# Products of spectra in an H3 layer with SwiGLU: instructions of 2560 elements against 5120 with a repeated row

## The chip, the core and the metric

The kernel runs on one core of one Trainium2 chip. The time is the device time of one execution in microseconds; lower is better. The kernel before was run three times: 264.83, 265.25 and 281.7 us, median 265.25 us. The profile shows one further execution of its own.

## What is computed

A sequence of 2048 tokens with 640 channels goes through two layers, each behind a layer norm and with a residual. The first is an H3 layer: `k` goes through a causal filter of four taps and is multiplied with `v`; the product is convolved along the sequence with a filter as long as the sequence (by FFT in the reference), gets a skip term, and is multiplied with the normed `q`. The second is a SwiGLU of width 1728.

```python
k_shift = sum(k_pad[:, t:t + S, :] * shift_k[:, ks - 1 - t][None, None, :] for t in range(ks))
kv = k_shift * v
y_f = rfft(kv padded to 2S) * rfft(ssm_k padded to 2S)
y = irfft(y_f)[:S].astype(bfloat16) + kv * ssm_D
h = q + layernorm(q) * y
n = layernorm(h)
out = h + (silu(n @ w_gate) * (n @ w_up)) @ w_down
```

## The kernel before

The sequence is cut into four blocks of 512 tokens. For block j, `kv` and the filter's piece `g` are brought into an odd-frequency spectrum of length 1024 by matmuls with the cosine and sine matrix `WF` (`transform`; products in PSUM, taken out by ACT or DVE at L364, the upper half of the frequencies made by one DVE sum, L410 or L439 to L445). A spectrum is a tile `S` of 128 partitions x 2 x 4 x 640 in bf16: two halves of the frequencies, in each two rows of cosine and two of sine parts. `X[j]` is the spectrum of `kv`, `G[j]` that of the filter's piece. `window` joins `G[j]` and `G[j-1]` to `H[j]` in two sums; for block 2 one of them is a DMA with accumulation issued by POOL (`S<-S`, L279).

The output spectrum of block j is A = X[0]H[j] + X[1]H[j-1] + ... + X[j]H[0], with complex products. `mac` makes one of these: m03 stands for the product of X[0] for block 3, m13 for that of X[1], and so on. `inverse` brings A back by matmuls with `WI` (L874), a DVE instruction per row of 128 tokens multiplies by the normed `q` (L888), adds the residual (L901, or a POOL DMA for blocks 1 and 2) and takes the sum for the second norm. `turn_h` norms the rows (ACT L803 or DVE L800) and transposes them (by DMA for blocks 1 to 3, L915). Then comes the FFN of the block: gate and up products on PE (L986, L1063), silu and copy on ACT (L1046, L1052), their product on DVE (L1054, here called a gate), the product with `w_down` on PE (L1106), and, for blocks 0 to 2, an accumulating POOL DMA of each row of tokens into the output (L1113).

The first norm of blocks 0, 1 and 3 is computed by POOL in 14 small instructions (L759 to L783) from sums that ACT takes (L750, L792); POOL's queue also issues the accumulating DMAs (L279) and part of the weight loads (L955). All other loads and transposes are issued by SP.

Nothing is scheduled at run time. The program first lists some 925 operations with what they read and write; `ORDER` is a list of their numbers, and each engine's queue is what the list leaves of its operations, in that order. A number -n-1 takes the other engine for an operation that has one (an eviction on DVE in place of ACT, a load by POOL in place of SP). Buffers are handed out along the same list from the counts in `SLOTS`: 8 tiles `S`, 11 tiles `big` of 5120 bytes a partition (blocks of x, v, k and g, turned tiles, weights, and scratch `scr`), 5 rows `row`, 4 pairs of gate tiles `sg`, 4 PSUM tiles `ps`. A buffer's next user waits for its last reader.

`mac` in the kernel before, for the first product of a block (L721 to L726) and for the others (L729 to L741): `part(sin)` is the cosine (0) or sine (1) part of both halves, 2 x 1280 elements.

```python
# first: six instructions of 2560 elements
t = X.part(1) * H.part(1);  u = X.part(1) * H.part(0)
A.part(0) = X.part(0) * H.part(0);  A.part(1) = X.part(0) * H.part(1)
A.part(0) -= t;  A.part(1) += u
# others: four pairs of 2560 elements, b a scratch tile of big
for xs, hs, dst, f in ((0, 0, 0, add), (0, 1, 1, add), (1, 1, 0, sub), (1, 0, 1, add)):
    b = X.part(xs) * H.part(hs);  A.part(dst) = f(A.part(dst), b)
```

For m11, `ADDP` lets the second pair's sum be an accumulating DMA (`S<-big`, L279). The products of block 0 (m00) are made in two pieces of 1280 elements by the first form.

Of the kernel before, what the change touches and what calls it, by code (L numbers as in the profile page):

```python
# [52 lines left out]
MERGE = ()  # L53
# [55 lines left out]
SLOTS = {'S': 8, 'big': 11, 'kT': 0, 'tT': 1, 'row': 5, 'sg': 4, 'ps': 4, 'sm': 6}  # L109
# [104 lines left out]
def kernel(ctx: ExitStack, tc: tile.TileContext, A_q, A_k, A_v, A_shift_k, A_ssm_k, A_ssm_D, B_x,  # L214
# [6 lines left out]

    slots = SLOTS
    shape = {"S": ([P, 2, 4, D], BF16), "U": ([P, 2, 4, D], BF16), "big": ([P, R * D], BF16), "kT": ([P, KT, R, PAD + P], BF16), "tT": ([P, NC_FULL, BLK], BF16),
# [476 lines left out]
    def mac(A, X, H, first, pieces=((0, 1),), adds=(), at=None):  # L700

        if at in MERGE:
            merged(A, X, H, first, [a for a in adds if isinstance(a, int)])
# [619 lines left out]
```

## Time and profile before

| | |
|---|---|
| runs, us | 264.83, 265.25, 281.7 |
| profiled execution, us | 268.25 |
| its span, first to last instruction, us | 266.5 |
| PE, DVE, ACT, POOL busy, us | 252.7, 205.6, 170.1, 86.8 |
| granted TensorE clock | 1.00 in all slices |
| moved by DMA | 46.38 MB, of it 12.13 MB by POOL's queue |

The profile's times are those of the profiled execution, which took 268.25 us, 3.0 us more than the median of the runs. Busy times of one engine are a union: matmuls overlap, so their mean duration times their number is more than PE's busy time. Where a group's row has idle time, it is time in which its engine stood still ahead of it, with what ended most of it. In the timeline, a start of the next instruction ahead of the end of the one before is normal on DVE: the engine's instructions overlap at their ends.

### The profile page before, as it was taken

Reading aid. Unit: us, or ns where it says so; the run is one execution under the profiler, and the core shown is the slowest. Engines: PE = TensorE matmul, PEld = TensorE weight load, DVE = VectorE, ACT = ScalarE, POOL = GpSimd, SP = SyncE. Lnnn points to the kernel's source line nnn. Section 1 sums busy time; section 2 is a strip of 40 time slices with the busy share of each in tenths; the row PEclk is TensorE's granted clock in tenths of the full one; section 3 lists DMA queues with packets and bytes.
Section 4 is the critical chain, followed back from the end, with each engine's and each line's share of the span. In section 5 each row is a group of like instructions: output and inputs, shape, how many; then the busy total and the mean of one; then the engine's idle time right before and its main releaser. Section 6 shows DMA issues by size and latency. Waiting matters only on the chain.

```text
span 266.5 us, 4771 instructions
## 1 busy us (share of the span) xinstructions
PE 252.7 (95%) x1800; PEld 153.9 (58%) x1818; DVE 205.6 (77%) x300; ACT 170.1 (64%) x291; POOL 86.8 (33%) x121
## 2 busy tenths in 40 slices
PE   8999989899999969799999999999999999999994
PEld 8977566555764537565644467644446764444662
DVE  5689999999895998899999999999999601112222
ACT  4978999995786955988956993445567223344100
POOL 7970000159716020443214220099972013000000
PEclk9999999999999999999999999999999999999999
DMA  7997999799799999999998589685399635300002
GB/s 259 370 213 163 259 312 237 198 311 241 212 189 105 167 245 224 243 242 179 227 210 162 123 255 184 167 133 141 87 189 304 137 75 57 43 0 0 2 26 72
DMA packets 65730, 46.38 MB, mean 174 GB/s; under 512 B 31030, under 2 KB 61244, under 8 KB 65708
## 3 DMA queue, kind: packets, MB, share of 16 engines
q1 hardware_dynamic: 59906, 33.94, 53.9%
q0 software_dynamic: 5792, 12.13, 24.7%
q8 instruction: 14, 0.23, 0.4%
q14 instruction: 8, 0.07, 0.1%
q10 hardware_dynamic: 10, 0.01, 0.0%
HBM read 30.01 MB, written 4.59 MB: 130 GB/s over the span
## 4 chain that ended last, share of the span: by engine, by line
PE 32%; DVE 27%; DMA 12%; POOL 6%; issue 6%; ACT 2%; SPq 2%; DVEq 0%; POOLq 0%; ACTq 0%
PE ps L1106 15%; PE ps L986 13%; DMA S<-S 8%; DVE big L739 6%; DVE S L740 5%; DMA out_dram<-big 3%; PE ps L1063 3%; DVE S L712 3%; DVE row L888 2%; SPq L461 2%; DVE tT L1054 1%; DMA big<-in_B_w_gate_dram 1%; DVE big L712 1%; DVE S L822 1%; POOL sm L782 1%
## 5 line engine op out<-in xcount | busy, mean ns | idle before, releaser
L986 PE MATMUL ps<-big,big 128*128 128x512 bf16 x465 | 107.0, 379 | 1.1 <-ACT sg L1052 0.3
L986 PEld LDWEIGHTS <-big 128*128 128x128 bf16 x480 | 46.7, 98 | 52.6 <-issue 0.5
L1106 PE MATMUL ps<-wd,tT 128*128 128x320 bf16 (+2 forms) x416 | 60.6, 299 | 3.3 <-DVE tT L1054 1.4
L1106 PEld LDWEIGHTS <-tT 128*128 128x128 bf16 x416 | 40.5, 98 | 20.8 <-issue 2.3
L1046 ACT ACTIVATE sg<-ps 128x1024 bf16<-128x1024 f32 (+1 forms) x28 | 27.1, 969 | 33.7 <-PE ps L986 26.5
L375 PE MATMUL ps<-big,WF 128*128 128x320 bf16 x240 | 39.6, 299 | 2.5 <-ACT big L364 1.3
L740 DVE TENSOR_TENSOR S<-S,big 128x2560 bf16<-128x2560 bf16 x23 | 34.3, 1492 | 1.4 <-DMA S<-big 0.7
L739 DVE TENSOR_TENSOR big<-S,S 128x2560 bf16<-128x2560 bf16 x23 | 34.1, 1483 | 0.6 <-DMA out_dram<-big 0.6
L375 PEld LDWEIGHTS <-WF 128*128 128x128 bf16 x240 | 23.1, 97 | 15.5 <-issue 4.2
L1054 DVE TENSOR_TENSOR tT<-sg,sg 128x1024 bf16<-128x1024 bf16 (+1 forms) x25 | 16.0, 642 | 19.9 <-ACT sg L1052 19.9
L1052 ACT CAST sg<-ps 128x1024 bf16<-128x1024 f32 (+1 forms) x25 | 23.7, 948 | 6.6 <-PE ps L986 4.3
L750 ACT ACTIVATE row<-big 128x640 bf16<-128x640 bf16 x32 | 23.8, 749 | 5.3 <-DMA big<-in_A_q_dram 3.2
L364 ACT CAST S<-ps 128x320 bf16<-128x320 f32 (+1 forms) x38 | 19.9, 567 | 5.2 <-PE ps L375 4.8
L1113 POOL DMA_DIRECT2D out_dram<-row x12 | 12.0, 1078 | 24.9 <-ACT row L1112 24.9
L1112 ACT CAST row<-ps 128x640 bf16<-128x640 f32 x12 | 8.1, 696 | 17.0 <-PE ps L1106 16.6
L803 ACT ACTIVATE row<-big,sm 128x640 bf16<-128x640 bf16 x20 | 17.9, 920 | 0.0
L364 ACT ACTIVATE big<-ps 128x640 bf16<-128x640 f32 (+1 forms) x25 | 16.0, 669 | 2.6 <-PE ps L375 2.5
L955 POOL DMA_DIRECT2D big<-in_B_w_gate_dram x8 | 8.3, 1040 | 26.3 <-DVE S L740 10.8
L1063 PE MATMUL ps<-big,big 128*128 128x512 bf16 x57 | 14.4, 379 | 0.5 <-DVE row L888 0.3
L712 DVE TENSOR_TENSOR big<-S,S 128x2560 bf16<-128x2560 bf16 (+1 forms) x10 | 12.1, 1217 | 3.3 <-DMA S<-S 3.2
L279 POOL DMA_DIRECT2D big<-row x8 | 6.9, 863 | 21.4 <-DVE row L888 11.0
L874 PEld LDWEIGHTS <-WI 128*128 128x128 bf16 x96 | 9.2, 98 | 6.4 <-issue 1.1
(107 smaller groups left out, 327.8 us busy)
## 6 DMA issues: line engine op xcount, KB each, us to landing
big<-in_B_w_up_dram SPq DMA_DIRECT2D x17, 320.0 KB, 4.4
big<-in_B_w_gate_dram SPq DMA_DIRECT2D x16, 320.0 KB, 5.3
big<-in_A_q_dram SPq DMA_DIRECT2D x4, 640.0 KB, 5.7
big<-in_A_v_dram SPq DMA_DIRECT2D x4, 640.0 KB, 6.3
big<-in_A_ssm_k_dram SPq DMA_DIRECT2D x4, 640.0 KB, 7.9
big<-in_B_w_gate_dram POOLq DMA_DIRECT2D x8, 320.0 KB, 5.2
big<-in_B_w_up_dram POOLq DMA_DIRECT2D x7, 320.0 KB, 5.6
wd<-in_B_w_down_dram SPq DMA_DIRECT2D x1, 2080.0 KB, 13.7
```

The costliest lines, as they stand in the source:

```text
L364: (lambda: nc.scalar.activation(dst(), src(), ACT.Copy, scale=2.0)) if twice else (lambda: nc.scalar.copy(dst(), src())),
L375: nc.tensor.matmul(ap(ps)[:, h, 0:NH], w, ap(src)[:, r, h * NH:(h + 1) * NH], start=(first and i == 0), stop=(last and i == len(rs) - 1), ...
L712: return lambda: f(*(x() for x in args))
L739: nc.vector.tensor_mul(flat2(b), X.part(xs), H.part(hs))
L740: f(A.part(dst), A.part(dst), flat2(b))
L750: act(825, lambda r=r, junk=junk: nc.scalar.activation(ap(junk), ap(x)[:, r, :], ACT.Square, scale=D ** -0.5, accum_out=sm(s, 1)[:, r:r + ...
L986: nc.tensor.matmul(of(ps, i), ap(w)[:, k, off:off + P], ap(hT)[:, k, lo:lo + n], start=(k == 0), stop=(k == KT - 1))
L1046: act(1010 if wide else 600, lambda: nc.scalar.activation(of(sg), of(*gate), ACT.Silu), [(gate[0], gate[1] + i) for i in range(m)], [sg])
L1052: op = plan.add("act", 1010 if wide else 590, lambda: nc.scalar.copy(of(co), of(*up)), psu + [sg], [co] + tt, (), ("dve", 1230 if wide els ...
L1054: op.rest = dve(690 if wide else 420, lambda: nc.vector.tensor_mul(to(), of(sg), of(co)), [sg, co], tt)
L1063: nc.tensor.matmul(ap(ps)[:, i, :], ap(w)[:, k, off:off + P], ap(hT)[:, k, :], start=(k == 0), stop=(k == KT - 1))
L1106: nc.tensor.matmul(ap(ps)[:, hf, to:to + n], t, ap(wd)[:, c, col + (hf - hs[0]) * NH:col + (hf - hs[0]) * NH + n], start=(c == order[0]), ...
```

## The change

Three constants are changed. `MERGE` names the nine products of blocks 1 to 3, which so go through `merged` (in the program before too, but not called there). `SLOTS` gets one wide buffer `U` of 10240 bytes a partition, and two `big` fewer. `ORDER` is written anew, since the numbers change (925 operations become 924) and the sequence with them.

```diff
-MERGE = ()
+MERGE = ((1, 0), (1, 1), (2, 0), (2, 1), (2, 2), (3, 0), (3, 1), (3, 2), (3, 3))
...
 ORDER = [
-    1, 22, 0, 2, 4, 5, 6, 23, 25, 16, 3, 13, 7, 11, 26, 9, 28, 10, 12, 8, 14, 15, 27, 38, 17, 18, 19, 39, 36, 37, 134, 32, -34,
...
+    0, 2, 24, 1, 4, 5, 7, 10, 6, 23, 3, 13, 8, 14, 15, 11, 9, 16, 22, 12, 41, 19, 32, 38, 34, 20, 25, 33, 36, -40, 40, -38, 35,
...
-SLOTS = {'S': 8, 'big': 11, 'kT': 0, 'tT': 1, 'row': 5, 'sg': 4, 'ps': 4, 'sm': 6}
+SLOTS = {'S': 8, 'kT': 0, 'tT': 1, 'row': 5, 'ps': 4, 'sm': 6, 'big': 9, 'U': 1, 'sg': 4}
```

What `merged` does, shortened; `rows(b)` is the whole tile as 2 x 2 x 1280, and `by(sin)` is one part of X with each half's 1280 elements read twice by a step of 0:

```python
def by(sin):
    return lambda: X.part(sin).unsqueeze(2).broadcast_to([P, 2, 2, 2 * D])
def times(T, sin):                      # 5120 elements
    return lambda: v.tensor_mul(rows(T.b), by(sin)(), rows(H.b))
T = Spec(new("U"), H.swapped)
if first:
    times(T, 1);  times(A, 0)
else:
    U = Spec(new("U"), H.swapped);  times(U, 0)
    v.tensor_add(rows(A.b), rows(A.b), rows(U.b))      # rows(U.b)[:, :, ::-1] if A and H hold cosine and sine the other way round
    times(T, 1)
v.tensor_sub(A.part(0), A.part(0), T.part(1))          # 2560 elements
v.tensor_add(A.part(1), A.part(1), T.part(0))
```

So a first product has four instructions (T, A, two sums) and another one five (U, +U, T, two sums). `U` and `T` take turns in the one buffer. `merged` takes only whole numbers from `ADDP`, and the entry for m11 is a pair, so the sum of m11 is made by DVE and its DMA is gone.

The new order as the queues see it, from the end of the inverse of block 0 to m02 (numbers of the new program in brackets):

| queue | before | after |
|---|---|---|
| POOL | norm 0, pairs, copy L554, two `T<-T` (block 2), DMA sum of m11, norm 1, DMA sum of H2 | norm 0, one `T<-T` (block 1), pairs, copy L554 (399), norm 1 (278), DMA sum of H2 (434) |
| ACT | two of the eight sums for norm 1 among block 0, six behind the eviction of X1 and G2's first | all eight sums for norm 1 (270 to 277) between X0 and the kv rows of block 1 |
| DVE | norm, H1, m01 with X1's upper half, m11 with 3 gates, inverse 1 (L819), G2's upper half, L822, H2, gate, m02 among four L888 | H1, norm, m01 (261 to 264) with X1's upper half, G2's upper half (433), m11 U (265), H2 (435), +U, gate, T, two sums, gate, inverse 1 with kv rows of block 2 and two gates, three L888 and a gate, m02's A (466), the last L888, m02's T, gate, its sums |
| PE | G2 among FFN 0 | G2 ahead of FFN 0, but for one part |

Seven gates of FFN 0, 1 and 2 stand directly behind a 5120 in the new order: behind +U of m11, T of m02, U of m12, T of m03, +U of m13, +U and T of m33. The first loads of SP are in both k, x, v and g of block 0 and `WF`; then before: D, g1, x1, the minus matrices, k1; after: x1, g2, D, the minus matrices, g1, k1. The load of `w_down` (2080 KB) is issued ahead of k2 in place of behind it. POOL issues 5, 5 and 8 of the weight pieces of FFN 1, 2 and 3 in place of 7, 3 and 5.

72 rows, old and new, of the table ORDER are left out of this document.

## The prediction, made before the changed kernel was run

> **What bounds the kernel now.** I read the busy table and the 40 slices first, then the stages, then the chain that ended last.
>
> ```profile
> span 266.5 us, 4771 instructions
> PE 252.7 (95%) x1800; PEld 153.9 (58%) x1818; DVE 205.6 (77%) x300; ACT 170.1 (64%) x291; POOL 86.8 (33%) x121
> DVE  5689999999895998899999999999999601112222
> 20.00:120.00 100.00, 92.42 (x716) 58.06 (x722) 93.34 (x124) 82.76 (x149) 29.35 (x34) 1.00 1.06 223
> 120.00:218.00 98.00, 96.54 (x612) 55.18 (x619) 89.09 (x127) 60.32 (x93) 37.54 (x37) 1.00 0.78 175
> ```
>
> Columns of the stages: length, then busy time of PE, PEld, DVE, ACT, POOL. Two engines are full at once. DVE works without a break from 20 us to about 205 us and then is nearly done. PE is full all along; its idle time is 7.6 us between 20 and 120 us, 1.5 us between 120 and 218 us, and the start and the very end. The last third is PE alone (FFN of block 3), and it can't begin before the inverse transform of block 3 leaves DVE. So DVE's queue sets when PE's last part may start, and PE's idle time before that is all that any change on DVE can win: at most 7.6 us of 268.
>
> Where does DVE itself stand still? The chain shows it.
>
> ```profile
> 71.69 0.29 POOL sm L760
> 71.98 1.63 issue
> 73.62 13.26 DMA S<-S
> 86.91 1.49 DVE big L712
> ...
> DVE big L712 <- DMA S<-S: 3.2, 1, 3.2
> PE ps L1106 <- DVE tT L1054: 1.4, 2, 1.2
> PE ps L1106 <- ACT sg L1071: 1.2, 1, 1.2
> PE ps L471 <- DMA big<-in_A_ssm_k_dram: 1.2, 1, 1.2
> ...
> 96.79 0.72 PE L1106 MATMUL ps<-wd,tT 128*128 128x320 bf16 x4 [1.24 <-DVE tT L1054]
> 99.81 6.41 PE L1106 MATMUL ps<-wd,tT 128*128 128x320 bf16 x46 [1.22 <-ACT sg L1071]
> ```
>
> The one long stop of DVE behind the start-up is at 83.7 us: the second product of m02 needs H2, one half of which is an accumulating DMA (S<-S, line 279). That DMA was issued at 73.6 us, when the POOL norm of block 1 had ended (72.0 us) and DVE had made G2's upper half, and it took 13.3 us. DVE waits 3.2 us. PE's stalls on FFN 0's gates (L1054, L1071) lie right behind it, at 96 to 100 us.
>
> **The change part by part.** *The products.* Per non-first mac four pairs (product, sum) become U, +U, T of 5120 elements and two sums of 2560; per first mac six of 2560 become two and two. The elements are the same, except that the DMA sum of m11 comes back to DVE. So only the fixed share of an instruction can be won, for 24 fewer of them, and the price of that is in how close the starts stand, not in the durations.
>
> ```profile
> L740 DVE TENSOR_TENSOR S<-S,big 128x2560 bf16<-128x2560 bf16 x23 | 34.3, 1492 | 1.4 <-DMA S<-big 0.7
> L739 DVE TENSOR_TENSOR big<-S,S 128x2560 bf16<-128x2560 bf16 x23 | 34.1, 1483 | 0.6 <-DMA out_dram<-big 0.6
> L712 DVE TENSOR_TENSOR S<-S,big 128x1280 bf16<-128x1280 bf16 x4 | 3.1, 814 | 0.0
> L854 DVE TENSOR_TENSOR S<-big 128x1280 bf16<-128x1280 bf16 x4 | 3.1, 820 | 0.0
> ...
> 112.75 1.48 DVE L739 TENSOR_TENSOR big<-S,S 128x2560 bf16<-128x2560 bf16 x1
> 114.27 1.49 DVE L740 TENSOR_TENSOR S<-S,big 128x2560 bf16<-128x2560 bf16 x1
> 115.68 1.48 DVE L739 TENSOR_TENSOR big<-S,S 128x2560 bf16<-128x2560 bf16 x1
> ```
>
> 1280 elements take 0.814 us and 2560 take 1.483: 0.523 ns an element and 0.145 us fixed. So 5120 would take 1.483 + 2560 x 0.523 ns = 2.82 us. But starts follow each other after 1.41 us where the next does not need the result and after 1.52 us where it does (112.75, 114.27, 115.68). A pair costs 2.93, a mac of four pairs 11.72 us. With the same overlap a 5120 is followed after 2.75 us, or 2.85 us if waited for. U, +U and T are each waited for, because U and T share the one wide buffer: 3 x 2.85 + 1.41 + 1.52 = 11.48 us, 0.24 less. For five macs that is 1.2 us. m11 had seven instructions (10.2 us) and gets 11.48: 1.3 us more. A first mac had six starts of about 1.41 (8.45 us); now 2.75 + 2.85 + 1.41 + 1.45, the same. Sum: **+0.1 us**. Bounds: if the whole duration of each instruction dropped counted, 24 x 0.145 less 1.41 would be -2.1 us; from above comes the case that the repeated row is read one element at a time, a rival below. I take +0.1, since the spacings are measured on this very kind of instruction. Rows with a reversed step (L854) run at the rate of plain ones (820 against 814 ns), so the reversed operand of +U costs nothing more.
>
> [...]
>
> *The order.* The list is written anew. Read by the program's numbering, the sequences of PE and DVE are nearly the same from block to block, and three moves matter. First, POOL's queue: the norm of block 1 now comes right behind the small copy L554 and has the DMA sum of m11 no longer in front of it, and ACT's eight sums for it are moved ahead into X0 to k1.
>
> ```profile
> 38.80 0.31 POOL L554 COPY T<-T 64x30 bf16<-64x30 bf16 x1 [18.99 <-ACT row L750]
> 56.53 1.28 POOL L279 DMA_DIRECT2D S<-big  x1 [2.61 <-DVE big L734]
> 57.35 1.58 POOL L768 TENSOR_TENSOR sm<-sm 128x4 f32<-128x4 f32 x1
> ...
> 47.47 2.88 DVE L712 TENSOR_TENSOR big<-S,S 128x2560 bf16<-128x2560 bf16 x2
> 71.84 1.48 DVE L410 TENSOR_TENSOR S<-big,S 128x2560 bf16<-128x2560 bf16 x1
> ...
> DMA to landing us min/median/max: 11.4/12.3/13.3
> ```
>
> So the norm can start near 39 us, not 57. Second, G2's upper half on DVE (71.84 here) stands right behind m01. From m01's start at 47.5: T and A 5.6, X1 1.4, two sums 2.9, G2 1.4, end at 58.8. The DMA sum of H2 can then be issued near 59 and lands near 72 (12.3 us). Third, m02 comes behind the first three rows of the inverse of block 1. Its first product: 58.8 + m11 and H2's other half (2.8 + 1.4 + 2.8 + 2.8 + 2.9) + inverse (2 x 1.4 + 3 x 0.74) + four gates of 0.6 + four kv products of 0.4 = about 80.5 us. The landing is 8 us ahead of it, so DVE's wait goes: **-3.2 us**. What hides it is that slack of 8; without it the wait is back. Next late would be PE's own work, but it has 7.6 us of idle time in that stretch, so I count the gain in full. Bounds: -3.2 to 0, and a loss through POOL (a rival).
>
> *The tail of block 3.* Between X3's last instruction and the inverse DVE now has 14 instructions of 25.0 us (six long, four short, four gates: 6 x 2.8 + 4 x 1.45 + 4 x 0.6), and POOL's norm of block 3 has 14 steps beside them.
>
> ```profile
> 183.06 1.44 POOL L782 TENSOR_SCALAR sm<-sm 128x4 f32<-128x4 f32 x1
> 184.58 1.32 POOL L783 TENSOR_TENSOR sm<-sm 128x4 f32<-128x4 f32 x1
> 17.02 0.20 POOL L783 TENSOR_TENSOR sm<-sm 128x4 f32<-128x4 f32 x1
> 201.28 0.81 DVE L888 SCALAR_TENSOR_TENSOR row<-row,ps 128x640 bf16<-128x640 bf16 x1
> 209.60 5.17 SPq L915 DMA_TRANSPOSE big<-row  x4
> big<-row SPq DMA_TRANSPOSE x12, 4.2
> 218.60 10.74 PE ps L986 x49
> out_dram<-row POOLq DMA_DIRECT2D x12, 160.0 KB, 4.2
> ```
>
> A POOL step takes 0.20 us where DVE works on small or PSUM operands (17 us) and 1.3 to 1.45 beside DVE's long products: it ends with the DVE instruction. So the norm ends after about 25 us, where it took 18. Behind it stand FFN 1's four output sums and two weight loads of 0.9 us each; the outputs free the `row` buffers that the inverse needs, 4.2 us after issue: the fourth at 25 + 5.4 + 4.2 = 34.6, plus ACT's 0.9, against a fourth L888 wanted at 34.3. **+0.8 us** (bounds 0 and 2). This counts, because the transposes of block 3 end at 214.8 and land 4.2 us later, just when FFN 3 begins (218.6).
>
> ```profile
> GB/s 259 370 213 163 259 312 237 198 311 241 212 189 105 167 245 224 243 242 179 227 210 162 123 255 184 167 133 141 87 189 304 137 75 57 43 0 0 2 26 72
> big<-in_B_w_gate_dram SPq DMA_DIRECT2D x16, 320.0 KB, 5.3
> ```
>
> *Loads and buffers.* g2 is loaded at the start: 640 KB ahead of the minus matrices and k1, some 2 us later for these at the first slices' 259 to 370 GB/s, while PE's 1.2 us wait for g2 goes: taken as 0 (-1.2 to +2). `big` falls from 11 to 9, but the products took one or two of the 11; one weight set less is ahead. No row of PE's waits names a weight load, so 0; without that cover a late set costs a landing, 5.3 us, once.
>
> **Sum**: 0.1 - 3.2 + 0.8 = -2.3 us. The profiled execution took 268.25 us (span 266.5 and 1.75 around it): 265.95. It lies 3.0 above the median 265.25, so the forecast is 265.25 - 2.3 = **263.0 us**.
>
> **The rivals.** (1) *The wait goes and nothing comes of it*: PE's stalls at 96 to 100 us have causes of their own (transfers, ACT) and DVE's 3.2 us are waited away again. 265.25 + 0.1 + 0.8 = 266.2.
>
> (2) *Gates behind long products*, the case on the slower side. In the new order seven FFN gates (L1054) stand directly behind a 5120. Where ACT and PE stand ready, each comes 1.33 us later than behind a 2560, and PE has four PSUM tiles to bridge it. If PE pays, DVE's gain counts for nothing: 265.25 + n x 1.33; five of seven give 271.9, all seven 274.6, and from four on it is over 2% slower. For it: PE has already waited for gates (1.4 and 1.2 us above). Against it: PE needs 4.4 us for a gate's 20 matmuls (10.74 us for 49 in FFN 3), longer than one product.
>
> (3) *POOL's norm of block 1 is stretched.* If its 14 steps fell beside 5120s alone, they would take 14 x 2.8 = 39 us from 39 on; H2's sum would be issued at 78 and land at 92, DVE would wait 11 instead of 3.2 us: 265.25 + 8.1 + 0.9 = 274.2. Against it: from 39 to 47 us DVE runs instructions under 0.9 us. [...]
>
> (4) *The repeated row costs the fast rate.*
>
> ```profile
> L651 DVE TENSOR_TENSOR big<-ps,big 128x640 bf16<-128x640 f32 x5 | 4.1, 822 | 2.2 <-PE ps L632 2.2
> L658 DVE TENSOR_TENSOR big<-big,big 128x640 bf16<-128x640 bf16 x11 | 5.0, 478 | 0.0
> ```
>
> At the rate of a PSUM operand (822 - 145 ns for 640, 1.06 ns an element) a product takes 5.6 us, 2.75 more; 18 of them make +49.5: about 315 us. Against it: the inner run is 1280 plain elements, as L712's.
>
> (5) *PE's gaps before 120 us close* to the 1.5 us that it has behind: 265.25 - 6.1 = 259.2. It needs every queue to fit better at once.
>
> **How the numbers follow.** Forecast 0.36 (its own range 260.5 to 265.5), (1) 0.15, (2) 0.30, (3) 0.06, (4) 0.03, (5) 0.10. 2% is 5.3 us, about what a measurement of this kernel can tell from no change. Faster: (5) and the forecast's edge, 0.11. Slower: (2) from four gates on 0.26, (3) 0.05, (4) 0.03: 0.34. Within: 0.55. The range goes from 259.0, (5) and the lowest bounds, to 274.5, (2) with all gates and (3).
>
> **What would show it.** Right: a 5120 of 2.8 us and starts 2.75 to 2.85 apart; S<-S issued near 59 us and no DVE wait for it; DVE busy for about 205 us as before; L888 of block 3 some 2 us earlier. Wrong: a wait of DVE for S<-S of over 3 us, POOL steps of 2.7 us near 50 us, PE waiting for L1054 or ACT's silu for it by several us, or products of 5 us.

## The result and the profile after

The changed kernel takes 273.6 us, the median of four runs (272.42, 273.37, 273.83, 273.96); the kernel before, run beside it, 265.5 us. The ratio is **1.027, 95% interval 1.022 to 1.032: slower**. The forecast was 263.0 us and no difference. Ratios below are to runs of the kernel before on the same chip and leave out the longer executions that come now and then (the kernel before took 265.07 to 279.29 us in 17 runs on one chip), so they can differ from a quotient of medians; where they do, the ratio counts.

The page of the profiled execution (273.96 us, span 272.3):

```profile
span 272.3 us, 4738 instructions
...
PE 256.9 (94%) x1818; PEld 156.6 (58%) x1818; DVE 206.8 (76%) x282; ACT 168.7 (62%) x285; POOL 90.9 (33%) x121
...
DVE  5689977999993999999989999999996701202322
...
PEclk9999997999997999999999999999999999999999
```

DVE works about as long as before (206.8 against 205.6 us), so the products are not where the time went. DVE has gaps near 40 us, which is new, and near 85 us, where it stood before too, but less (a slice of 0.3 now, of 0.5 before). New as well are two slices in which the granted clock of TensorE isn't full: before, it was 1.00 everywhere. PE is busy 4.2 us longer for the same matmuls.

The products did what was forecast. L677 writes the products U, T and, in a first mac, A; L692 is +U with the rows read in reverse. Groups, then DVE's timeline (start, duration, instruction):

```profile
L677 DVE TENSOR_TENSOR U<-S,S 128x5120 bf16<-128x5120 bf16 x15 | 42.3, 2818 | 0.1
L692 DVE TENSOR_TENSOR S<-S,U 128x5120 bf16<-128x5120 bf16 x4 | 11.3, 2824 | 0.1
```

```profile
52.24 2.82 DVE L677 TENSOR_TENSOR U<-S,S 128x5120 bf16<-128x5120 bf16 x1
54.98 2.82 DVE L677 TENSOR_TENSOR S<-S,S 128x5120 bf16<-128x5120 bf16 x1
57.72 1.48 DVE L410 TENSOR_TENSOR S<-big,S 128x2560 bf16<-128x2560 bf16 x1
...
85.80 0.82 DVE L888 SCALAR_TENSOR_TENSOR row<-row,ps 128x640 bf16<-128x640 bf16 x1 [4.17 <-PE ps L874]
...
90.05 2.82 DVE L677 TENSOR_TENSOR S<-S,S 128x5120 bf16<-128x5120 bf16 x1
```

2.82 us for 5120 elements with a row read twice, 2.74 us from start to start, no loss for the reversed row of +U (2824 against 2818 ns). But m01 starts at 52.24 us, before at 47.47. And DVE's wait for S<-S is gone, since POOL issues this DMA ten us earlier than before:

```profile
63.72 1.26 POOL L279 DMA_DIRECT2D S<-S  x1 [14.14 <-DMA T<-T]
```

Another wait follows in its place: 4.17 us of DVE for PE, which end at 85.8.

What waits, by engine (total, times, longest):

```profile
ACT row L803 <- DMA out_dram<-row: 3.3, 3, 2.0
PE ps L986 <- DMA big<-in_B_w_gate_dram: 3.3, 1, 3.3
...
PE ps L641 <- POOL pairs L1180: 2.2, 3, 1.5
```

None of these waits was among the long ones before. They lie in three places.

**(a) The start of block 1.** POOL's timeline, the last `pairs` of before first, then the changed kernel:

```profile
11.29 1.68 POOL L1180 TENSOR_SCALAR pairs<-row,taps 128x64 bf16<-128x64 bf16 x4
...
17.67 2.14 POOL L1180 TENSOR_SCALAR pairs<-row,taps 128x64 bf16<-128x64 bf16 x4
```

```profile
27.97 0.92 POOL L563 DMA_DIRECT2D T<-T  x1 [10.54 <-ACT big L473]
28.95 10.47 POOL L1180 TENSOR_SCALAR pairs<-row,taps 128x64 bf16<-128x64 bf16 x8
43.99 0.22 POOL L554 COPY T<-T 64x30 bf16<-64x30 bf16 x1 [4.57 <-PE ps L641]
```

Eight small instructions that make the filter taps of block 1 (`pairs`) stand behind a transfer that waits until 28 us for work of block 0. They then take 10.5 us beside DVE's work on block 0: one takes 5.90 us, during which DVE runs instructions of 1280 elements without a break, the last 1.76 us beside a sum of 2560, the other six 0.43 to 0.92 us. Before, they were done by 20 us at 0.44 to 0.45 us each and one at 0.89 us. PE's filter products L641 wait for them, then DVE.

**(b) Weights of FFN 0** (the expectations below call these the weights of FFN 1; they belong to FFN 0). SP's timeline, PE's, and the stretches around PE's stop (length, busy time of PE, PEld, DVE, ACT, POOL, granted clock):

```profile
71.66 2.54 SPq L330 DMA_DIRECT2D big<-in_A_ssm_k_dram  x1
74.24 2.83 SPq L955 DMA_DIRECT2D big<-in_B_w_gate_dram  x3
```

```profile
81.67 2.31 PE L986 MATMUL ps<-big,big 128*128 128x512 bf16 x5 [3.33 <-DMA big<-in_B_w_gate_dram]
83.77 1.92 PE L874 MATMUL ps<-big,WI 128*128 128x320 bf16 x8
85.52 1.24 PE L986 MATMUL ps<-big,big 128*128 128x512 bf16 x5
86.60 1.25 PE L874 MATMUL ps<-big,WI 128*128 128x320 bf16 x8
```

```profile
78.30:81.60 3.30, 0.04 (x2) 0.00 (x0) 3.30 (x4) 3.30 (x5) 0.88 (x1) 1.00 1.20 295
81.60:85.30 3.70, 3.63 (x12) 1.64 (x13) 0.02 (x1) 0.26 (x1) 0.00 (x0) 0.54 0.81 151
```

The gate weights that PE needs at 78.3 us are issued behind block 3's filter g3 (L330), which is needed only later, and land at 81.6. PE stands 3.3 us, and then runs 3.7 us at 0.54 of its clock: five matmuls take 2.31 us that take 1.24 a moment later. DVE's wait of 4.17 us for PE (above) comes from both.

**(c) The tail of block 3.** POOL's norm and output sums, then ACT and PE behind them:

```profile
174.50 1.68 POOL L768 TENSOR_TENSOR sm<-sm 128x4 f32<-128x4 f32 x1
176.25 2.81 POOL L759 TENSOR_SCALAR sm<-sm 128x4 f32<-128x4 f32 x1
...
198.31 1.85 POOL L1113 DMA_DIRECT2D out_dram<-row  x2
```

```profile
201.92 0.92 ACT L803 ACTIVATE row<-big,sm 128x640 bf16<-128x640 bf16 x1 [1.98 <-DMA out_dram<-row]
...
205.41 1.52 PE L1106 MATMUL ps<-wd,tT 128*128 128x320 bf16 x10 [1.85 <-ACT sg L1046]
```

Five of POOL's 14 steps now last 2.6 to 2.8 us, each beside a DVE instruction of 5120. The norm takes 23.8 us, the output sums behind it go out at 198.3 (192.9 was the end of the norm before), ACT waits for the rows that they free, and PE waits for ACT. PE's stop behind ACT stands in f1_loads and f6_row5 below (2.0 and 1.9 us) and is gone where ACT has no such wait (b_norm3_dve, f2_all, f5_row9).

### The profile page after: what moved, and what is told of

Same layout as the page of the kernel before. It is cut to its first block, busy times and chain, and to the rows that moved or that the text cites. A ratio compares the mean times of both kernels' runs of the same rounds, so it can differ in the third digit from the quotient of the medians.

```text
span 272.3 us, 4738 instructions
## 1 busy us (share of the span) xinstructions
PE 256.9 (94%) x1818; PEld 156.6 (58%) x1818; DVE 206.8 (76%) x282; ACT 168.7 (62%) x285; POOL 90.9 (33%) x121
## 4 chain that ended last, share of the span: by engine, by line
PE 46%; DVE 25%; POOL 11%; DMA 9%; ACT 4%; issue 3%; SPq 1%; DVEq 0%; POOLq 0%; ACTq 0%
PE ps L986 17%; PE ps L1106 16%; DVE U L677 6%; PE ps L375 5%; DMA T<-T 3%; PE ps L1063 2%; DMA out_dram<-row 2%; DVE S L690 2%; DVE S L677 2%; DMA big<-in_B_w_gate_dram 2%; PE ps L874 2%; DMA row<-in_A_ssm_D_dram 2%; POOL pairs L1180 2%; PE ps L641 2%; POOL sm L759 2%
## 5 line engine op out<-in xcount | busy, mean ns | idle before, releaser
L986 PE MATMUL ps<-big,big 128*128 128x512 bf16 x480 | 108.7, 382 | 3.3 <-DMA big<-in_B_w_gate_dram 3.3
L1046 ACT ACTIVATE sg<-ps 128x1024 bf16<-128x1024 f32 (+1 forms) x28 | 26.7, 962 | 34.6 <-PE ps L986 34.2
L677 DVE TENSOR_TENSOR U<-S,S 128x5120 bf16<-128x5120 bf16 x15 | 42.3, 2818 | 0.1
L375 PE MATMUL ps<-big,WF 128*128 128x320 bf16 x240 | 39.2, 298 | 2.7 <-ACT big L364 1.6
L375 PEld LDWEIGHTS <-WF 128*128 128x128 bf16 x240 | 23.3, 97 | 15.5 <-issue 4.8
L1051 DVE TENSOR_TENSOR tT<-sg,ps 128x1024 bf16<-128x1024 bf16 (+1 forms) x4 | 4.3, 1086 | 26.4 <-PE ps L986 16.0
L1113 POOL DMA_DIRECT2D out_dram<-row x12 | 13.6, 1401 | 31.6 <-ACT row L1112 31.6
L803 ACT ACTIVATE row<-big,sm 128x640 bf16<-128x640 bf16 x20 | 17.9, 938 | 3.3 <-DMA out_dram<-row 3.3
L364 ACT CAST S<-ps 128x640 bf16<-128x640 f32 (+1 forms) x35 | 18.8, 590 | 1.4 <-PE ps L375 1.3
L888 DVE SCALAR_TENSOR_TENSOR row<-row,ps 128x640 bf16<-128x640 bf16 x16 | 12.8, 816 | 6.9 <-PE ps L874 6.4
L955 POOL DMA_DIRECT2D big<-in_B_w_up_dram x8 | 9.6, 1287 | 21.3 <-ACT row L803 11.8
L364 ACT ACTIVATE big<-ps 128x640 bf16<-128x640 f32 (+1 forms) x22 | 14.1, 709 | 3.8 <-PE ps L375 3.8
L1180 POOL TENSOR_SCALAR pairs<-row,taps 128x64 bf16<-128x64 bf16 x20 | 15.6, 805 | 0.1
L1063 PE MATMUL ps<-big,big 128*128 128x512 bf16 x60 | 14.4, 379 | 0.7 <-ACT sg L1046 0.7
L955 POOL DMA_DIRECT2D big<-in_B_w_gate_dram x10 | 12.0, 1475 | 7.3 <-DVE S L535 6.2
```

Of the source, the lines that this page charges most:

```text
L364: (lambda: nc.scalar.activation(dst(), src(), ACT.Copy, scale=2.0)) if twice else (lambda: nc.scalar.copy(dst(), src())),
L375: nc.tensor.matmul(ap(ps)[:, h, 0:NH], w, ap(src)[:, r, h * NH:(h + 1) * NH], start=(first and i == 0), stop=(last and i == len(rs) - 1), ...
L677: return lambda: v.tensor_mul(rows(T.b), x(), rows(H.b))
L803: nc.scalar.activation(ap(row), ap(x)[:, r, :], ACT.Identity, bias=sm(s, 5)[:, r:r + 1], scale=sm(s, 4)[:, r:r + 1])
L955: return lambda: q.dma_start(out=ap(w)[:, :, to:to + n], in_=cols(src, lo, n))
L986: nc.tensor.matmul(of(ps, i), ap(w)[:, k, off:off + P], ap(hT)[:, k, lo:lo + n], start=(k == 0), stop=(k == KT - 1))
```

## The experiments

**Theory 1**: the loss is made by the places (a), (b), (c) of the new order and by the fewer `big`, and PE's clock behind its stops adds to it; the merged products cost nothing. **Theory 2**: the long products themselves cost it, by what is queued behind them. The kernels of one section differ only in what their diff shows; diffs show a queue's part of `ORDER` by what the operations are. Where the text prices a step by two medians, the difference of the two ratios, times 265.5 us, stands beside it as the price by the ratios.

| kernel | us | ratio to before, 95% |
|---|---|---|
| changed kernel | 273.6 | 1.022 to 1.032 |
| a_pairs_first | 270.98 | 1.014 to 1.028 |
| c_big10 | 276.29 | 1.034 to 1.050 |
| b_norm3_dve | 271.52 | 1.016 to 1.032 |
| g_fill | 271.8 | 1.010 to 1.024 |
| e_new_order_pairs | 277.04 | 1.030 to 1.048 |
| d_old_order10, d2, d3 | 272.2, 272.62, 272.73 | 1.019 to 1.030, 1.014 to 1.035, 1.014 to 1.027 |
| d4_old_row_first | 269.38 | 1.011 to 1.024 |
| f1_loads | 267.82 | 1.005 to 1.012 |
| f2_all; again | 265.92; 265.6 | 1.000 to 1.005; 0.996 to 1.001 |
| f3_start | 269.05 | 1.007 to 1.014 |
| f4_row9 | 269.58 | 1.013 to 1.021 |
| f6_row5 | 265.35 | 0.994 to 1.000 |
| **f5_row9** | **262.53** | **0.981 to 0.991** |
| g5_pairs | 270.98 | 1.015 to 1.023 |
| h_before_norm3 | 270.11 | 1.000 to 1.011 |

### The three places, one at a time

```diff
 # a_pairs_first: POOL's queue
-T<-T of block 1, pairs, pairs, copy L554, norm 1
+pairs, pairs, T<-T of block 1, copy L554, norm 1
```

> The changed kernel with one edit: on POOL the last two chunks of `pairs` (L1180) stand ahead of the small transfer T<-T (L563) and no longer behind it. Theory 1 (the loss comes from the new order and the fewer `big` buffers): POOL makes them before 28 us, PE no longer waits for pairs (2.2 us there), m01 starts near 48 in place of 52.2 us, and the time falls from 273.6 to 269 to 271. Theory 2 (the loss comes from the long products themselves): 273 to 274, since all products stay as they are; DVE makes up for a late start elsewhere.

Measured 270.98 us. m01's first product starts at 48.74, PE has no wait for `pairs`. The number falls in theory 1's range. (a) is worth 2.6 us by the medians and 1.6 by the ratios, whose intervals overlap, and not the 4.8 by which m01 was late. PE now comes to the late weights earlier and stands 3.94 us there.

```diff
 # c_big10
-diag = fixed([P, KT * 4, P], BF16, "diag")
+diag = (a view of the first 5120 bytes of U's room)
-'big': 9
+'big': 10
```

> The changed kernel with a tenth `big` (the diagonal matrices lie inside U's room), its order untouched. Theory 1: the gate weights of FFN 1 are issued earlier, PE's wait of 3.3 us for big<-in_B_w_gate_dram goes or falls under 1 us, DVE's 4.2 us for L888 near 86 us falls, while the late `pairs` stay: 270 to 272. Theory 2: 273 to 274.

Measured 272.48 to 277.98, median 276.29: theory 1's 270 to 272 is missed, and by the ratio this is slower than the changed kernel, for a reason that stays open. PE's wait for the gate weights stands:

```profile
PE ps L986 <- DMA big<-in_B_w_gate_dram: 3.1, 1, 3.1
```

That part of theory 1 falls: the weights aren't late for want of a buffer, they are late because of what SP issues ahead of them.

```diff
 # b_norm3_dve
-LN1DVE = (2,)
+LN1DVE = (2, 3)
```

> The changed kernel with the norm of block 3 on DVE in place of POOL, at the same place of the list. Theory 1: DVE pays 2.2 us, POOL's output sums of FFN 1 go out 8 to 15 us earlier, ACT's 3.3 us and PE's stops at 200 to 210 us shrink: 270.5 to 272.5. Theory 2: 275 to 276, by what DVE pays.

Measured 271.52, in the middle of theory 1's range. Its interval overlaps that of the changed kernel, so the time alone shows no sure gain. In the trace ACT's wait for out_dram<-row is gone, and PE's 1.85 us behind it.

```diff
 # f1_loads: a_pairs_first, 10 big, and SP's queue (T = T<-T, up/gate = weights of FFN 0)
-T, gate, T, T, output 0, up, gate, up, v2, up, up, gate, g3, gate, gate, gate, up
+T, gate, up, gate, T, T, output 0, up, v2, up, up, gate, gate, gate, gate, up, g3
```

> The changed kernel with `pairs` ahead of T<-T on POOL (as in a_pairs_first), 10 `big`, and SP's queue put right: two weight loads of FFN 0 stand ahead of the transfers T<-T that they were queued behind, and block 3's filter stands behind the gate weights of FFN 1. Theory 1: PE's wait of 3.9 us for these weights near 75 us and the half clock behind it go: 266 to 269. If the transfers are bound by their rate and not by the queue, the wait stays and the time is 270 to 271. Theory 2: 273.

Measured 267.82, as theory 1 had it: PE's wait for gate weights falls, the clock is 1.00 in all stretches.

```profile
PE ps L986 <- DMA big<-in_B_w_gate_dram: 0.8, 1, 0.8
```

Against a_pairs_first this is 3.2 us (3.4 by the ratios). c_big10 showed no gain from a tenth `big`, and f6_row5 below has no such wait with nine, so it is the order.

```diff
 # f2_all: f1_loads and
-LN1DVE = (2,)
+LN1DVE = (2, 3)
 # SP at the start
-x1, g2, D, minus matrices    (behind ACT's sums of block 0)
+D and the minus matrices ahead of these sums
```

> f1_loads with the norm of block 3 on DVE and, at the start, the load of D and the minus matrices ahead of ACT's sums of block 0, so that SP isn't held up by a `row`. Theory 1: m00 starts 2 us earlier (near 20.3), the tail is shorter by 2 to 4 us: 262 to 266. Theory 2: 273 or more.

Measured 265.92, and 265.6 the second time: the loss is undone with all nine merged products in place. The start didn't improve (m00 at 22.59 us, not 20.3), so the 1.9 us against f1_loads (1.5 by the ratios) are put down to the norm. f3_start tried the start by itself:

```diff
 # f3_start: f2_all, with the first 121 operations in the order of the kernel before
```

> f2_all with the old order up to the first product of m00 (block 0's start as in the kernel before), the new one behind it. f2_all starts m00 near 22.6 us, the kernel before at 20.3. If the start is what separates f2_all from a gain: m00 near 20.5, 263.5 to 265. If DVE makes it up or ACT's sums for norm 1, which now fall behind m00's start, hold up G0 and G1: 266 to 268.

Measured 269.05, the second alternative and a little beyond it: PE waits 2.6 us for ACT (`PE ps L375 <- ACT S L364`) and has 0.83 of the clock in 20 to 30 us. An order that is good with one continuation is not good with another. And the norm's edit by itself, on the kernel before:

```diff
 # h_before_norm3: the kernel before, with
-LN1DVE = (2,)
+LN1DVE = (2, 3)
```

> The kernel before with the norm of block 3 on DVE, nothing else: it tells how much of f2_all's time comes from that edit alone. Its POOL steps beside products of 2560 take 1.3 to 1.45 us and the norm 18 us, so the outputs of FFN 1 are not late: DVE's 2.2 us are a loss: 266 to 268. If the tail of the kernel before hangs on POOL as well: 263.5 to 265.

Ratio 1.006 (1.000 to 1.011): no gain there. So the edit is no gain of its own; it repairs what the long products do to POOL.

### What PE's stop costs beyond itself

```diff
 # g_fill: in the group of FFN 0 that waits at 78.3 us
+for _ in range(14):
+    nc.tensor.matmul(ps, ident, WF[512 columns], start=True, stop=True)   # overwritten by the group
 for k in range(KT):
     nc.tensor.matmul(ps, w[k], hT[k], start=(k == 0), stop=(k == KT - 1))
```

> The changed kernel with 14 idle matmuls (identity times WF, 512 columns, into the PSUM tile that the next group overwrites) ahead of the group of FFN 0 that waits 3.3 us for its gate weights. Nothing arrives earlier; only PE has work while it waits. If the half clock behind this stop is set by PE's standing still: the granted clock stays at 1.00 between 80 and 90 us, the two groups behind the stop take 1.24 and 1.25 us in place of 2.31 and 1.92, and the time falls by 1 to 2 us, to 271.5 to 272.5. If the clock falls for another reason: 273 to 274, with 0.83 in that stretch.

Measured 271.8, with no transfer earlier: 1.8 us less by the medians, 2.8 by the ratios, whose intervals just overlap. PE's timeline (one of the 14 has no record):

```profile
77.70 3.19 PE L989 MATMUL ps<-WF,ident 128*128 128x512 bf16 x13
81.21 1.25 PE L991 MATMUL ps<-big,big 128*128 128x512 bf16 x5 [0.33 <-DMA big<-in_B_w_gate_dram]
82.30 1.25 PE L874 MATMUL ps<-big,WI 128*128 128x320 bf16 x8
```

The weights arrive as late as before, but the groups behind take 1.25 us at once, at a clock of 1.00. So with PE at work in the stop no half clock followed; in the changed kernel's trace it made the stop of 3.3 us cost some 1.7 us more than it lasted (2.31 and 1.92 less 1.24 and 1.25). That PE's standing still is the cause is not proved by this one trace: c_big10 has a stop of 3.1 us at the same place, no idle matmuls, and a clock of 1.00 behind it. In g_fill the other stop, 2.2 us in three pieces behind `pairs`, still has 0.83 of the clock behind it (40 to 50 us).

The length of a stop doesn't decide whether the clock falls. By windows of the traces (of 0.5 us in the changed kernel, a_pairs_first, d_old_order10 and e_new_order_pairs, of 10 and 20 us in the others), the clock fell to half in or behind stops of 0.8 us (d_old_order10, at 52.9 us), 1.5 (`pairs`, the changed kernel), 2.6 (f3_start), 2.9 (d_old_order10), 3.0 (d2, e_new_order_pairs, g5_pairs), 3.3 (the changed kernel), 3.9 (a_pairs_first) and 4.8 us (f4_row9). It stayed full behind stops of 1.2 us (the kernel before), 1.5 (`pairs`, c_big10), 2.6 (d3), 3.1 (c_big10), 3.2 (b_norm3_dve) and 3.8 (e_new_order_pairs, the stop for gate weights). In the windows of 0.5 us it stayed at half for 3.4 us each time, and for 6.8 us in e_new_order_pairs. In the wider windows the half clock isn't seen by itself; taken as half, 0.83 of 10 us is 3.4 us, and g5_pairs comes to 6.8. No run shows what decides between a fall and none.

Executions of one kernel differ in it too. The four runs of the changed kernel had a mean granted clock of 0.987, 0.987, 0.994 and 0.999 and took 273.96, 273.83, 273.37 and 272.42 us. By these runs the half clock is worth about 1.5 us of this kernel's time; at a clock of 0.999 it is still some 7 us slower than the kernel before (272.42 against 265.5).

### Order against products

```diff
 # e_new_order_pairs: the new order, MERGE = (), each merged product replaced by its pair or pairs
-'big': 9, 'U': 1
+'big': 11
```

> The new order with the old products: pairs of instructions of 2560 elements at the places where the merged ones stand, 11 `big`, no wide buffer, m11's sum by DVE. Theory 1: the late `pairs` stay (m01 near 52), the late weights go with 11 `big`, and POOL's last norm is back at some 18 us: 268 to 270, slower than before by over 1%. Theory 2: without the long products the time is that of the kernel before, 265 to 266.

Measured 277.04: slower than the changed kernel. Theory 2 had 265 to 266 and is wrong for this order; theory 1 had 268 to 270 and missed too. Its late `pairs` shrank without an edit to them: the eight took 7.6 us in place of 10.5, PE's list has no wait for them, and m01 starts at 49.6. Weights are as late with 11 `big` (3.8 us), which again speaks against the buffers, and there is a new wait, 3.5 us of DVE:

```profile
DVE big L739 <- DMA S<-big: 3.5, 1, 3.5
```

A pair writes its product to a scratch `big`. L739 of m23 reads no part of X3, so what it waits for must be its scratch, which X3's accumulating DMA still reads. The merged form has its own U and can't run into this.

```diff
 # d_old_order10: the list of before, MERGE and U as changed, 10 big
 # d2_old_order_k_first: the same, on SP
-up, gate, filter of block 2, gate          (up/gate = weights of FFN 0)
+filter of block 2, gate, up, gate
```

> The old order with the merged products: the list of before, each pair of products replaced by one of 5120 at the place of the first, one `U` and 10 `big` (the diagonal matrices, used only in the first block, lie inside U's room to make space for the tenth); eleven loads or first uses of a buffer stand a few places later, where ten buffers ask for it. Theory 1: no late `pairs`, m01 near 47.5, DVE's wait for S<-S much as before (some 3 us): 264.5 to 267. Theory 2: the long products cost their price in any order: 271 to 273.

> The old order with the merged products and 10 `big` once more, with one edit: block 2's filter K (L330) is loaded ahead of the first of the FFN weights that it had been queued behind on SP. In the kernel without this edit PE stood 2.93 us for that filter at 39 to 42 us, with two stretches at half the granted clock behind it. Theory 1 (order, loads and the clock behind PE's stops make the loss): the stop falls to about 1.2 us as before, the clock stays full, 265.5 to 268. Theory 2 (the long products cost their price in any order): 271 to 273 as without the edit.

Measured 272.2 and 272.62. The stop for the filter did fall to 0.8 us and the time didn't follow: theory 1's number is missed twice, theory 2's holds. Why is seen on DVE, in the kernel before and then in d2:

```profile
77.46 1.48 DVE L712 TENSOR_TENSOR S<-S,S 128x2560 bf16<-128x2560 bf16 x1
...
81.49 1.47 DVE L712 TENSOR_TENSOR big<-S,S 128x2560 bf16<-128x2560 bf16 x1
82.89 0.80 DVE L888 SCALAR_TENSOR_TENSOR row<-row,ps 128x640 bf16<-128x640 bf16 x1
...
86.91 1.49 DVE L712 TENSOR_TENSOR big<-S,S 128x2560 bf16<-128x2560 bf16 x1 [3.21 <-DMA S<-S]
```

```profile
86.24 2.83 DVE L677 TENSOR_TENSOR U<-S,S 128x5120 bf16<-128x5120 bf16 x1 [3.71 <-DMA S<-S]
88.99 0.81 DVE L888 SCALAR_TENSOR_TENSOR row<-row,ps 128x640 bf16<-128x640 bf16 x1
```

Before, two products of m02 and the fourth L888 run ahead of the first instruction that needs H2's accumulated half. U reads both halves, so nothing of m02 can run ahead, and the fourth L888 stood behind U. PE in d2 waits for that L888 and has 0.83 of the clock behind it:

```profile
89.86 0.70 PE L375 MATMUL ps<-big,WF 128*128 128x320 bf16 x4 [3.00 <-DVE row L888]
```

POOL may add to it: its norm takes 57.4 to 77 us beside the long products (three steps of 2.6 to 2.7 us), S<-S is issued behind it at 76.9, before at 73.6.

```diff
 # d3_old_norm1_dve: d2 with
-LN1DVE = (2,)
+LN1DVE = (1, 2)
```

> The old order with the merged products and 10 `big` (as in d2_old_order_k_first), with the norm of block 1 on DVE in place of POOL. In d2_old_order_k_first POOL's norm took 57.4 to 77 us beside products of 5120 (steps of 2.6 to 2.7 us), S<-S was issued behind it at 76.9 us, DVE waited 3.7 us for it, and PE stood 3.0 us with half the clock behind that. If the long products do their harm in the old order through POOL's norm: S<-S is issued at 72 to 74 us, DVE's wait falls to 0 to 2 us, PE's stop goes, and with 2.2 us more on DVE the time is 267 to 269.5. If the harm comes from DVE's own queue (gates behind long products): 272 to 274.

Measured 272.73: the second alternative, so taking the norm off POOL gains nothing here. POOL was free, but S<-S was issued at 76.94 all the same, because G2's upper half on DVE, which it also needs, came at 75.15 behind products and norm (71.84 before). DVE's wait stayed at 3.4 us.

```diff
 # d4_old_row_first: d2, DVE's queue
-U of m02, fourth L888
+fourth L888, U of m02
```

> d2_old_order_k_first with one instruction moved: the fourth L888 of block 1's inverse stands ahead of m02's U on DVE, and no longer behind it. In the kernel before DVE makes two products of m02 and the fourth L888 ahead of the product that waits for H2's accumulated half; U needs both halves, so the wait of 3.7 us comes earlier and L888 was queued behind it, with PE behind L888 (3.0 us, half the clock after it). Theory (the merged product's wait for both halves is what costs the old order): PE's 3.0 us stop goes, the clock stays full, DVE still waits some 4 us for S<-S: 267.5 to 270. If the stop isn't what sets the time: 272 to 273.

Measured 269.38: PE's 3.0 us are gone, the clock is full, 3.2 us won by the medians, 1.8 by the ratios, whose intervals overlap. So a quarter to a half of the old order's loss was one row behind U; the other 3.4 to 4.7 us are not traced to one place (DVE still waits 2.2 us for S<-S; fewer `big` and eleven moved operations are in it).

### Rows against the norm, and the products in an order that suits them

```diff
 # f4_row9: f1_loads, and room for rows in place of a big
-'row': 5, 'big': 10
+'row': 9, 'big': 9
 # (G2's evictions and transforms some places later, as nine big ask)
 # f5_row9: and SP's queue (names as in f1_loads)
-T, gate, up, gate, T, T, output 0, up, v2, up, up, gate, gate, gate, gate, up, g3
+T, gate, T, T, up, gate, output 0, up, v2, up, up, gate, gate, gate, gate, up, g3
 # (and the third group's gate weights ahead of those of two others; G2 again as in f1_loads)
 # f6_row5: f5_row9 with
-'row': 9
+'row': 5
```

> f1_loads with 9 `big` and 9 `row` in place of 10 and 5 (POOL keeps the norm of block 3, SP's and POOL's order as in f1_loads; eight evictions and transforms of G2 stand some places later, as nine `big` ask). In f1_loads ACT waits 4.8 us in four pieces for output sums of FFN 1 that are issued behind POOL's norm (they free the rows). If these rows set the tail: ACT's waits for out_dram<-row go, the fourth L888 of block 3 comes 2 to 3 us earlier, and without the 2.2 us that DVE pays in f2_all the time is 263.5 to 266. If POOL's norm itself sets it: 267 to 268 as f1_loads.

> f4_row9 with the loads put so that nine `big` hold up nothing: two weight loads of FFN 0 stand ahead of the first output (and no longer ahead of T<-T), the third group's gate weights ahead of two other groups, block 3's filter behind them; G2 as in the changed kernel. In f4_row9 PE stood 4.8 us at 52 to 57 us for a `big` of G2, which hid what the rows gave. Expected: that stop goes, PE's wait for gate weights near 75 us is under 2 us, no wait of ACT for out_dram<-row: 263.5 to 266, with every merged product kept. If the rows gave nothing: 267 to 269.

> f5_row9 with 5 `row` in place of 9, nothing else. If the rows that wait for FFN 1's output sums behind POOL's stretched norm set the tail: ACT's waits for out_dram<-row come back (3 to 5 us), the last L888 of block 3 comes 2 to 4 us later, and the time is 265 to 267. If they set nothing: 262 to 263.

f4_row9 took 269.58: ACT's wait for the rows was gone, but PE stood 4.8 us at 52 to 57 us behind an eviction of G2 for which no `big` was free, so its time tells nothing of the rows. f5_row9 took **262.53**, f6_row5 265.35: the four rows are worth 2.8 us (3.0 by the ratios). ACT's first L803 of block 3 in f6_row5, then in f5_row9:

```profile
194.50 0.92 ACT L803 ACTIVATE row<-big,sm 128x640 bf16<-128x640 bf16 x1 [2.00 <-DMA out_dram<-row]
```

```profile
191.12 1.73 ACT L803 ACTIVATE row<-big,sm 128x640 bf16<-128x640 bf16 x2
```

The page of f5_row9:

```profile
span 261.2 us, 4739 instructions
...
PE   8999998899999999999999999999999989999995
...
PEclk9999999999999999999999999999999999999999
...
PE 88%; ACT 6%; DMA 2%; SPq 1%; issue 1%; DVE 0%; DVEq 0%; ACTq 0%
```

PE is full, the clock too, and the chain that ended last is PE for 88% of the span. This version beats both kernels: 1.4% faster than the kernel before (0.9 to 1.9%). The loads and rows of the kernel before were not worked over in the same way, so the 1.4% is not the price of the merged products.

```diff
 # g5_pairs: the order of f5_row9, MERGE = (), pairs at the places of the merged products
-'row': 9, 'big': 9, 'U': 1
+'row': 5, 'big': 11
```

> The order of f5_row9 with the old products: pairs of 2560 at the places of the merged ones, 11 `big`, 5 `row`, no U. To be read against f6_row5, which has the same order and rows with the merged products. If the merged products are worth something by themselves (starts spaced 2.75 to 2.85 against two of 1.41 to 1.52, m11 and the first macs aside): 1 to 2 us slower than f6_row5. If they are worth nothing: the same; and as POOL's last norm is stretched less here, it can be 1 to 2 us faster.

Measured 270.98 against f6_row5's 265.35, more than either alternative. It has the wait of e_new_order_pairs again (L739 for S<-big, 3.5 us), with PE 3.0 us behind it and 0.70 of the clock at 200 to 210 us. So most of the 5.6 us is probably that wait and what follows from it, which no run took away by itself, and what a merged product is worth by its length stays open.

## Why the prediction was right or wrong

*Products, +0.1*: right. 2.82 us were forecast and measured, the spacing too, and DVE's busy time is 1.2 us above that of before, with m11's sum (1.4 us) back from the DMA.

*DVE's wait for S<-S, -3.2*: the mechanism was right, and S<-S was issued at 63.72 us, which is the forecast 59 plus the 4.8 us by which m01 was late. The gain itself was lost at once: DVE then stood 4.17 us for PE at nearly the same place.

*Start, "m01 at 47.5"*: the step that failed first. The table of queues in front of the prediction shows `pairs` behind T<-T on POOL, but the prediction priced only norm 1 and H2's sum in that queue. What a queue's head waits for (work of block 0, until 28 us) was in no sum. Worth 2.6 us (a_pairs_first; 1.6 by the ratios).

*Loads and buffers, 0*: this step failed too, and it was the dearest. The case named there, a late weight set, is what happened (a stop of 3.3 us, 5.3 were named), but for another reason than the nine `big`: with ten and eleven the wait stayed. The prediction looked at the bytes and buffers of the loads, not at what stands ahead of the one that is needed next. Worth 3.2 us (a_pairs_first to f1_loads; 3.4 by the ratios) and, with f5_row9's better order, 2.5 more (f1_loads to f6_row5, a `big` less; 2.9 by the ratios).

*Tail, +0.8*: right mechanism, mis-sized. The stretched norm was forecast at 25 us and took 23.8; the rows behind it cost 2.8 us (f5_row9 against f6_row5). The term doesn't follow from its own working either: 34.6 plus ACT's 0.9 less 34.3 is 1.2, not 0.8.

*Left out*: PE's clock, for which the prediction has no term. g_fill puts the half clock behind one stop at about 1.8 us by the medians; it is contained in the prices above.

The four prices add up to what lies between the changed kernel and f5_row9, 2.6 + 3.2 + 2.5 + 2.8 = 11.1 us, but they must, since each is measured from one kernel of this chain to the next; another sequence of edits could share them out otherwise. With all of them taken off the kernel takes 262.5. That this is near the forecast 263.0 doesn't confirm the forecast's sum: f5_row9 has other loads and four more rows than the kernel that was forecast.

*Rivals.* In time (2), 271.9 to 274.6, and (3), 274.2, came nearest, both by chance. (2): no wait of PE for a gate behind a product is among its long ones. Its general form, that something short stands behind a long product, is true in the old order, where it was a row (d4_old_row_first). (3), POOL's norm 1 stretched, didn't happen in the new order, where it ran at 44 to 50 us, but did in the old one (57.4 to 77 us in d2). (4) is refuted by 2.82 us. (5), PE's gaps close, is what f5_row9 does for the larger part: of 7.6 us of idle time between 20 and 120 us it has 2.8 left, and the 259.2 are not reached.

## What to carry to other kernels

A longer instruction in the place of two waits for the operands of both, and it holds up what is queued behind it for twice as long (2.74 us from start to start against 1.41 here). Work of another engine beside it can be held up too: the longest steps of POOL's norm took 2.6 to 2.8 us here, before 1.3 to 1.5. So look first for what the shorter ones ran ahead of, and move that. Where an order is written anew, walk through each in-order queue, the load queues included, and ask of every head what it waits for and of every wait who stands behind it; the bytes and the busy times tell nothing of that. A stop of the matmul engine of some 3 us can be dearer than it looks, because half the clock may follow it (1.7 us more behind 3.3 us in the changed kernel, nothing behind 3.1 us in c_big10), so the few transfers that end in such a stop are worth placing by hand.

## What the runs showed of the hardware

- Stops of PE of 0.8 to 4.8 us were followed by half the granted clock in some traces and not in others, and the longer stop wasn't always the one that was followed by it (3.8 us without, 2.6 us with). By windows of 0.5 us the half clock lasted 3.4 us, in e_new_order_pairs 6.8. With 14 idle matmuls in the stop the clock behind it was 1.00 (g_fill).
- POOL's small instructions took longer beside DVE's long ones. Of the last eight `pairs`, 0.44 to 0.89 us each before, one took 5.90 us in the changed kernel beside DVE instructions of 1280 elements without a break (in e_new_order_pairs the longest took 1.5 us). The longest steps of the norm of block 3 took 1.3 to 1.5 us beside instructions of 2560 elements and 2.6 to 2.8 us beside 5120.
- The repeated row of a step of 0 and the reversed row of +U took no longer than plain rows would by the forecast from 1280 and 2560 elements: 2818 and 2824 ns for 5120 elements, 2.82 us forecast.
